# Seven block products instead of eight for the down projection in the second token half, with stored operands and gate/up products chained in PSUM

## The chip, the cores and the metric

The kernel runs on one core of a Trainium2 chip. The metric is device time in microseconds (us): the median of 3 runs of the kernel before is 1944.34 us (1938.64 to 1944.6). The profile is of one further execution.

## The reference

One transformer block over S = 2048 tokens of width D = 576, in float32.

```python
x = x + ga * attention(layernorm(x) * (1 + ca) + sa)     # 32 heads, causal in 4 segments, with a memory
h = layernorm(x) * (1 + cb) + sb                          # 2048 x 576
g = silu(h @ w_gate)                                      # 576 x 4608
u = h @ w_up                                              # 576 x 4608
x = x + gb * ((g * u) @ w_down)                           # 4608 x 576
```

The change is in the last three lines, the feed-forward part. Every float32 operand of a matmul is split into a high part in a shorter format (fp32r) and a low part, the remainder, and a product of two such operands takes three matmuls: high by high, high by low, low by high.

## The kernel before

**Stages.** Projections and attention run first and are, but for one DMA queue, not touched. Then the feed-forward part runs as two token halves t of 1024 tokens (1024 = two blocks of L = 512). In each half it walks through p = 0 to 17: NPR = 18 *periods*, each for 256 of the 4608 hidden columns. The loop `for t`, `for p`, `for k` at the end of `block` writes out by hand, in program order, what each engine does. Each engine works through its own queue strictly in that order and waits where an operand is missing or a buffer is not yet free.

**Gate and up by seven products.** A period computes the gate (z = 0) and up (z = 1) parts of 256 columns by 1024 tokens, as 2 by 2 blocks with a seven-product scheme of the Strassen kind in place of eight block products. So a period has 14 *steps* k = 0 to 13, one product m each, in the order MO7. The seven token-side operands `y[:, o]` are made once for each half. The weight-side operands are sums of the four raw blocks: `load_o` brings the raw blocks, `sum_o` (L1059, POOL) makes three new blocks and overwrites one, `prep_w` (L1065 to L1067) makes the high part on ACT, the low part `wl` on DVE and a 32-row remainder on POOL. `prod` (L1082 to L1091) then issues seven 128x512 matmuls into a PSUM bank of tag "M", which has four banks. `step` and `fin` (L1098 to L1131) combine the products *outside* PSUM: DVE adds each bank to a running sum `tx` or `ty`; gate blocks go through Silu on ACT; up blocks are multiplied with the gate blocks, and the result is split into `ah` (ACT) and `al` (DVE).

**Down by eight products.** `down` (L1141 to L1158) takes the split result of the period before and the split down weights (`load_d`, `prep_d`), and for each of eight token tiles issues 2 x 6 matmuls of 128x288 into a pair of banks of tag "dn" (two such pairs); DVE adds each pair into an accumulator `acc` (L1155). The eight pieces are spread over steps 4 to 11. The very last period's down pieces stand behind the loop.

**Beside it.** While half 0 runs, the generator `prep2` (L969 to L1038) normalises half 1's tokens, makes its seven token-side operands and stores them in HBM; it is advanced once in each of steps 4 to 13. `load_y` brings them into `y` during the last period of half 0.

**What sets the order around the change.** PSUM has 8 banks: four "M" and two pairs "dn". A list `later` holds the DVE and POOL halves of an operand's preparation and issues them one step after its ACT half. SP issues almost every DMA in program order.

## Time and profile before

| | |
|---|---|
| median of 3 runs | 1944.34 us (1938.64 to 1944.6) |
| profiled execution | span 1946.8 us; the page gives no other time for it |
| PE (matmul) busy | 1901.2 us, 98% of the span |
| DVE, POOL, ACT busy | 1533.1, 1020.6, 824.8 us (79%, 52%, 42%) |
| first gate/up product starts, last down matmul ends | 659.16 us, 1942.82 us |
| mean TensorE clock granted | 0.993 of full |

PE is TensorE, DVE VectorE, ACT ScalarE, POOL GpSimd, SP the engine that issues DMAs. A group's row gives the line, the engine, the operation, the tiles it writes and reads, the count, and then busy time in all and the mean of one in ns. Matmul records overlap: each lasts longer than the distance from its start to the next one's start, and that distance is what it costs PE. The same holds for DVE.

### The profile page before, as it was taken

Reading aid. Unit: us, or ns where it says so; the run is one execution under the profiler, and the core shown is the slowest. Engines: PE = TensorE matmul, PEld = TensorE weight load, DVE = VectorE, ACT = ScalarE, POOL = GpSimd, SP = SyncE. Lnnn points to the kernel's source line nnn. Section 1 sums busy time; section 2 is a strip of 40 time slices with the busy share of each in tenths; the row PEclk is TensorE's granted clock in tenths of the full one; section 3 lists DMA queues with packets and bytes.
Section 4 is the critical chain, followed back from the end, with each engine's and each line's share of the span. In section 5 each row is a group of like instructions: output and inputs, shape, how many; then the busy total and the mean of one; then the engine's idle time right before and its main releaser. Section 6 shows DMA issues by size and latency. Waiting matters only on the chain.

```text
span 1946.8 us, 31901 instructions
## 1 busy us (share of the span) xinstructions
PE 1901.2 (98%) x11119; PEld 1593.1 (82%) x11119; DVE 1533.1 (79%) x3218; ACT 824.8 (42%) x1652; POOL 1020.6 (52%) x1396
## 2 busy tenths in 40 slices
PE   7999999999999899999999999999999999999999
PEld 4887865676766678888888888888888888888888
DVE  6575257878786999898898988979888888878886
ACT  2222256767667434344344343433333333333332
POOL 5322235455544866556565565556565564655551
PEclk9999999999999899999999999999999999999999
DMA  7776564444443332232222222174211211112111
GB/s 207 244 227 233 203 204 140 131 139 150 136 128 125 92 135 101 89 106 80 80 106 83 82 84 78 60 264 146 74 62 45 74 62 59 60 62 74 62 57 50
DMA packets 114354, 223.59 MB, mean 115 GB/s; under 512 B 22992, under 2 KB 40784, under 8 KB 112720
## 3 DMA queue, kind: packets, MB, share of 16 engines
q1 hardware_dynamic: 111936, 215.61, 34.2%
q0 software_dynamic: 576, 5.11, 0.7%
q8 instruction: 88, 1.44, 0.3%
q10 hardware_dynamic: 1680, 0.82, 0.2%
q14 instruction: 74, 0.61, 0.1%
HBM read 161.11 MB, written 60.36 MB: 114 GB/s over the span
## 4 chain that ended last, share of the span: by engine, by line
PE 88%; DVE 4%; DMA 4%; ACT 1%; issue 1%; POOL 1%; SPq 1%; POOLq 0%; ACTq 0%; DVEq 0%
PE M L1090 39%; PE pd L1152 23%; PE pp L93 4%; PE s L576 4%; PE av L596 4%; PE s L174 4%; PE pv L93 3%; PE pw L694 2%; DMA O<-in_wgu_dram 1%; DMA mD<-mr 1%; PE pn L765 1%; PE pm L429 1%; PE px L617 1%; PE pr L346 1%; DVE y L923 1%
## 5 line engine op out<-in xcount | busy, mean ns | idle before, releaser
L1090 PE MATMUL M<-y,wh 128*128 128x512 f32 x2520 | 792.0, 393 | 5.0 <-DVE cu L1106 2.1
L1090 PEld LDWEIGHTS M<-y,wh 128*128 128x128 f32 x2520 | 473.7, 188 | 101.7 <-issue 3.9
L1067 POOL TENSOR_TENSOR wh<-O,wh 32x128 fp32r<-32x128 f32 x504 | 296.6, 593 | 423.0 <-ACT wh L1065 271.3
L1090 PE MATMUL M<-y,wl 128*128 128x512 f32 x1008 | 394.7, 392 | 0.0
L1059 POOL TENSOR_TENSOR O<-O 128x384 f32<-128x384 f32 x288 | 315.4, 1095 | 75.0 <-DMA O<-in_wgu_dram 42.9
L1152 PE MATMUL pd<-dh,ah 128*128 128x288 f32 x1152 | 340.3, 295 | 0.2 <-DVE acc L1155 0.2
L1152 PE MATMUL pd<-dl,ah 128*128 128x288 f32 x1152 | 340.3, 295 | 0.0
L1152 PE MATMUL pd<-dh,al 128*128 128x288 f32 x1152 | 340.1, 295 | 0.0
L1110 ACT CAST ah<-sg 128x512 fp32r<-128x512 f32 x144 | 89.5, 621 | 547.8 <-DVE sg L1107 422.0
L1155 DVE TENSOR_TENSOR acc<-acc,pd 128x576 f32<-128x576 f32 x288 | 216.5, 752 | 111.8 <-PE pd L1152 108.4
L1066 DVE TENSOR_TENSOR wl<-O,wh 128x256 fp32r<-128x256 f32 x504 | 286.2, 568 | 6.0 <-ACT wh L1065 5.2
L179 DVE CUSTOM_DVE_ANT_0 junk<-s,tri 128x256 bf16<-128x256 f32 (+3 forms) x512 | 228.7, 487 | 77.2 <-PE s L174 69.8
L1065 ACT CAST wh<-O 128x384 fp32r<-128x384 f32 x504 | 242.8, 507 | 0.0
L1152 PEld LDWEIGHTS pd<-dl,ah 128*128 128x128 f32 x1152 | 217.4, 189 | 11.8
L1152 PEld LDWEIGHTS pd<-dh,ah 128*128 128x128 f32 x1152 | 216.7, 188 | 11.6 <-DVE acc L1155 0.6
L579 ACT ACTIVATE Pt<-s 128x512 f32<-128x512 f32 (+1 forms) x352 | 186.5, 559 | 88.1 <-PE s L576 72.0
L1152 PEld LDWEIGHTS pd<-dh,al 128*128 128x128 f32 x1152 | 216.6, 188 | 0.0
L1090 PEld LDWEIGHTS M<-y,wl 128*128 128x128 f32 x1008 | 190.0, 188 | 29.6
L1102 ACT ACTIVATE sg<-sg 128x512 f32<-128x512 f32 x144 | 91.2, 633 | 222.7 <-DVE sg L1101 222.7
L576 PE MATMUL s<-qs,ks 110*128 110x512 f32 (+2 forms) x384 | 150.5, 409 | 5.7 <-DMA qs<-mD 4.4
L174 PE MATMUL s<-ks,qs 108*128 108x256 f32 (+3 forms) x512 | 141.2, 327 | 3.3 <-DMA ks<-kD 1.4
L583 POOL TENSOR_SCALAR_AFFINE_SELECT Pt<-Pt 128x512 f32<-128x512 f32 x128 | 81.6, 648 | 100.6 <-ACT Pt L579 100.2
(428 smaller groups left out, 2836.6 us busy)
## 6 DMA issues: line engine op xcount, KB each, us to landing
O<-in_wgu_dram SPq DMA_DIRECT2D x72, 768.0 KB
ks<-kD SPq DMA_DIRECT2D x68, 216.0 KB
qs<-qD SPq DMA_DIRECT2D x68, 216.0 KB
kD<-fh SPq DMA_DIRECT2D x16, 512.0 KB
qD<-fh SPq DMA_DIRECT2D x16, 512.0 KB
yD<-st SPq DMA_DIRECT2D x28, 256.0 KB
y<-yD SPq DMA_DIRECT2D x7, 1024.0 KB
wml<-in_w_mod_dram SPq DMA_DIRECT2D x24, 216.0 KB
```

Of the source, the lines that this page charges most:

```text
L93: nc.tensor.matmul(ps, lhsT=a, rhs=b, start=(k == 0), stop=(k == 13))
L174: nc.tensor.matmul(bank[:, n * (h - h0):n * (h - h0) + n], lhsT=qst[b][0:108, h, 128 * i:128 * i + 128], rhs=kst[b][0:108, h // 2, 0:n], s ...
L179: nc.vector.tensor_tensor_reduce(junk[:, :n], bank[:, n * (h - h0):n * (h - h0) + n], tri[:, L - n:], 1.0, -3e38, op0=ALU.add, op1=ALU.max ...
L576: nc.tensor.matmul(bank[:, n * (g - h):n * (g - h + w)].rearrange("p (a b) -> p a b", a=w), lhsT=kst[u % NB][0:110, g // 2, 128 * j:128 * ...
L579: nc.scalar.activation(pt[:, h:h + per, :n], bank[:, :n * per].rearrange("p (a b) -> p a b", a=per), AF.Exp, scale=SCALE)
L1059: nc.gpsimd.tensor_tensor(o[:, d], o[:, a], o[:, b], op=op)
L1065: nc.scalar.copy(wh, o)
L1066: later.append(lambda: nc.vector.tensor_tensor(wl, o[:, 0:2], f32(wh[:, 0:2]), op=ALU.subtract))
L1067: later.append(lambda: nc.gpsimd.tensor_tensor(wh[32:64, 2], o[32:64, 2], f32(wh[32:64, 2]), op=ALU.subtract))
L1090: nc.tensor.matmul(bank, lhsT=a, rhs=b, start=(n == 0), stop=(n == 6))
L1152: nc.tensor.matmul(pd[:, h, :288], lhsT=a[:, tk], rhs=w[:, f, sl], start=(k == 0), stop=(k == 5))
L1155: nc.vector.tensor_tensor(o, o, pd[:, :, :288], op=ALU.add)
```

## The change

In words:

- **Down, half 1.** In periods 0 to 16 of half 1 `down` uses a seven-product scheme: seven products of 512 tokens by 288 columns with 128 hidden rows each, in 14 pieces of 6 matmuls (84 in place of 96), accumulated in seven accumulators `acc[1]` to `acc[7]`; DVE adds 14 pieces in place of 8. It needs sums of the split results, `sum_a` (4 DVE adds a period), seven `ah`/`al` in place of four, and seven `dh`/`dl` of 288 columns in place of two of 576. In half 0, and for half 1's last period, `plain` issues the same 96 matmuls as before, arranged by blocks. In the last period `comb` folds the seven accumulators into the four output blocks (5 adds on DVE, 3 on POOL, of 1152 elements).
- **Operands stored.** In half 0 POOL makes the weight sums as before, and the sums of the down weights (`sum_d`), and SP stores them to HBM (`oD`, `rD`, `wdD`). In half 1 they are loaded, and POOL does none of this. The third row block of the seven gate/up operands is prepared in one piece (`prep_r`: one ACT copy and one POOL subtraction of 896 columns for each z, in place of seven small ones), so `prep_w` covers 256 columns in place of 384.
- **Chained in PSUM.** Products of one z add up in three banks: A (two buffers) takes M1, then M6, M7 and M4 on top of it; ACT copies A to B after M1, and M2 is added on top of B; C takes M5, and later M3. ACT copies A out twice (`tb`, `tc`). The DVE additions into `tx` and `ty` go, and two of the four Silu inputs are read straight from PSUM. MO7 becomes 1, 5, 6, 2, 7, 4, 3. Operands are prepared 5 steps ahead (PF) in place of 7, with 7 buffers (WR) in place of 10.
- **Smaller moves.** `prep2` transposes into the "dn" banks and has one buffer `st` in place of two; residuals are loaded at steps given by RS; `vD` is stored from ACT's queue in place of POOL's; the host call sets a smaller DMA scratch (`dynamic_dma_scratch_size=1024`).

Cut to its core:

```diff
-WR = 10
+WR = 7
+PF = 5
+NSG = 8
+CH = (1, 1, 1, 1, 2, 1, 0, 1, 1, 1, 1, 2, 1, 0)
+CH0 = (0, 1, 1, 0, 1, 1, 0, 1, 0, 1, 1, 1, 0, 0)
+RS = {(0, 5): 2, (0, 6): 4, (0, 8): 3, (0, 10): 5, (1, 9): 2, (1, 11): 3, (1, 13): 4}
+KS = (0, 1, 2, 3)
+KA = ((5, 2), (6, 4), (7, 6), (3, 8))
+ASRC = {5: (1, 1), 6: (0, 0), 7: (0, 1), 3: (1, 0)}
...
-WW = (19, 23, 25, 26, 27, 29, 30)
+WW = (19, 23, 25, 27, 30)
...
+    wdD = [dr.tile([P, 7, 288], F32, tag=f"wd{p}", name=f"wd{p}") for p in range(NF // 2)]
+    oD = [[dr.tile([P, 4, 3, P], F32, tag=f"oD{p}_{z}", name=f"oD{p}_{z}") for z in range(2)] for p in range(NF // 2)]
+    rD = [[dr.tile([96, 7, P], F32, tag=f"rD{p}_{z}", name=f"rD{p}_{z}") for z in range(2)] for p in range(NF // 2)]
...
-                nc.gpsimd.dma_start(vD[s], vs[s])
+                nc.scalar.dma_start(vD[s], vs[s])
...
-    MO7 = (1, 2, 6, 7, 4, 5, 3)
+    MO7 = (1, 5, 6, 2, 7, 4, 3)
...
-            st = x2p.tile([P, 2, 256], F32R, tag="st", name="st", bufs=2)
+            st = x2p.tile([P, 2, 256], F32R, tag="st", name="st")
...
-                    pt = ps.tile([P, 4, P], F32, tag="M", name="pt", bufs=4)
+                    pt = ps.tile([P, 2, L], F32, tag="dn", name="pt", bufs=2)[:, 0].rearrange("p (a b) -> p a b", b=P)
...
+    def load_o(t, p, z):
         O[p, z] = o = opl.tile([P, 7, 3, P], F32, tag="O", name="O", bufs=2)
+        if t == 0:
+            nc.sync.dma_start(o[:, 0:4], wgu[p, z])
+        else:
+            nc.sync.dma_start(o[:, 1:4], wgu[p, z][:, 1:4])
+            nc.sync.dma_start(o[:, 0], oD[p][z][:, 0])
+            nc.sync.dma_start(o[:, 4:7], oD[p][z][:, 1:4])
+    def store_o(p, z):
+        nc.sync.dma_start(oD[p][z][:, 0], O[p, z][:, 0])
+        nc.sync.dma_start(oD[p][z][:, 1:4], O[p, z][:, 4:7])
+    def prep_r(t, p, z):
+        R[z] = r = wrp.tile([P, 7, P], F32R, tag="wr", name="wr")
+        if t == 1:
+            nc.sync.dma_start(f32(r[0:96]), rD[p][z])
+            return
+        o = O[p, z]
+        nc.scalar.copy(r[0:96], o[0:96, :, 2, :])
+        later.append(lambda: nc.gpsimd.tensor_tensor(r[32:64], o[32:64, :, 2, :], f32(r[32:64]), op=ALU.subtract))
...
-        o = O[p, z][:, SLOT[m]]
-        wh = wp.tile([P, 3, P], F32R, tag="wh", name="wh")
+        o = O[p, z][:, SLOT[m], 0:2]
+        wh = wp.tile([P, 2, P], F32R, tag="wh", name="wh")
-        later.append(lambda: nc.vector.tensor_tensor(wl, o[:, 0:2], f32(wh[:, 0:2]), op=ALU.subtract))
-        later.append(lambda: nc.gpsimd.tensor_tensor(wh[32:64, 2], o[32:64, 2], f32(wh[32:64, 2]), op=ALU.subtract))
+        later.append(lambda: nc.vector.tensor_tensor(wl, o, f32(wh), op=ALU.subtract))
-    def load_d(p, i):
-        RD[i] = r = rp.tile([P, D], F32, tag="d", name="dr_")
-        nc.sync.dma_start(r, wd[2 * p + i])
...
+    def load_d(t, p):
+        RW[p] = r = rp.tile([P, 7, 288], F32, tag="d", name="dr_")
+        if t == 0:
+            for f in range(2):
+                nc.sync.dma_start(r[:, 2 * f:2 * f + 2].rearrange("p a b -> p (a b)"), wd[2 * p + f])
+        else:
+            nc.sync.dma_start(r[:, :NS[p]], wdD[p][:, :NS[p]])
+    def mul_d(p, f):
+        v = RW[p][:, 2 * f:2 * f + 2].rearrange("p a b -> p (a b)")
+        nc.gpsimd.tensor_tensor(v, v, gbB, op=ALU.mult)
+    def sum_d(p, j):
+        r = RW[p]
+        d, a, b = ((4, 1, 0), (5, 3, 4), (6, 2, 5), (1, 3, 1))[j]
+        nc.gpsimd.tensor_tensor(r[:, d], r[:, a], r[:, b], op=ALU.subtract)
+    def prep_d(p, key, slot):
+        r = RW[p][:, slot]
+        dh = dp.tile([P, 288], F32R, tag="dh", name="dh")
+        dl = dp.tile([P, 288], F32R, tag="dl", name="dl")
+        nc.scalar.copy(dh, r)
+        later.append(lambda: nc.vector.tensor_tensor(dl, r, f32(dh), op=ALU.subtract))
+        DP[p % 2, key] = (dh, dl)
...
+        ops.append((R[z][0:96, SLOT[m]], y[0:96, o, 4]))
-            nc.tensor.matmul(bank, lhsT=a, rhs=b, start=(n == 0), stop=(n == 6))
-        return bank
-
-    T, SG, AC = {}, {}, {}
+            nc.tensor.matmul(bank, lhsT=a, rhs=b, start=(first and n == 0), stop=(n == 6),
+                             skip_group_check=not first)
...
+            SG[ij] = g = tmp("sg", NSG)
+            if add is None:
+                nc.scalar.activation(g, bank, AF.Silu)
+            else:
+                nc.vector.tensor_tensor(g, bank, add, op=ALU.add)
+                nc.scalar.activation(g, g, AF.Silu)
+        if add is None:
+            nc.vector.tensor_tensor(g, bank, g, op=ALU.mult)
+        else:
+            u = tmp("cu", 2)
+            nc.vector.tensor_tensor(u, bank, add, op=ALU.add)
+            nc.vector.tensor_tensor(g, u, g, op=ALU.mult)
+        AC[ij] = g
+    def copy_t(tag, bank):
+        T[tag] = t = tmp(tag, 2 if tag == "cu" else 1)
+        nc.scalar.copy(t, bank)
+    B = {}
+    def step(z, m):
+        if m == 1:
+            B["A"] = ps.tile([P, L], F32, tag="A", name="A", bufs=2)
+            B["B"] = ps.tile([P, L], F32, tag="B", name="B", bufs=1)
+        elif m == 5:
+            B["C"] = ps.tile([P, L], F32, tag="C", name="C", bufs=1)
+        bank = B["B" if m == 2 else "C" if m in (5, 3) else "A"]
+        prime = "set" not in B
+        prod(z, m, bank, m in (1, 5) or m == 2 and prime, m in (2, 4, 3))
+        if m == 1:
+            if prime:
+                copy_t("cu", bank)
+            else:
+                nc.scalar.copy(B["B"], bank)
+        elif m == 2:
+            fin(z, (0, 0), bank, T["cu"] if prime else None)
+            B["set"] = True
+        elif m == 6:
+            copy_t("tb", bank)
+        elif m == 7:
+            copy_t("tc", bank)
+            fin(z, (1, 1), B["C"], T["tc"])
+        elif m == 4:
+            fin(z, (1, 0), bank)
+        elif m == 3:
+            fin(z, (0, 1), bank, T["tb"])
+    def prep_a(par, m, src):
         ah = ap_.tile([P, L], F32R, tag="ah", name="ah")
         al = ap_.tile([P, L], F32R, tag="al", name="al")
+        nc.scalar.copy(ah, src)
+        later.append(lambda: nc.vector.tensor_tensor(al, src, f32(ah), op=ALU.subtract))
+        AP[par, m] = (ah, al)
+    def sum_a(j):
+        d, a, b, op = (((1, 1), (0, 1), (1, 1), ALU.add), ((0, 1), (0, 0), (0, 1), ALU.subtract),
+                       ((0, 0), (1, 1), (0, 0), ALU.subtract), ((1, 0), (1, 0), (0, 0), ALU.subtract))[j]
+        nc.vector.tensor_tensor(PA[d], PA[a], PA[b], op=op)
+    PA, acc, x11 = {}, {}, {}
+    NS = [7] * (NPR - 1) + [4]
+    def new_acc():
+        for m in range(1, 8):
+            acc[m] = accp.tile([P, 4, 288], F32, tag=f"acc{m}", name=f"acc{m}")
...
+    def down(t, p, c):
+        m, c = POS[c // 2], c % 2
+        ah, al = AP[p % 2, m]
+        dh, dl = DP[p % 2, m]
+        pd = ps.tile([P, 2, L], F32, tag="dn", name="pd", bufs=2)
+        for i in range(2):
+            tk = slice(128 * (2 * c + i), 128 * (2 * c + i) + 128)
+            for k, (a, w) in enumerate(((ah, dh), (ah, dl), (al, dh))):
+                nc.tensor.matmul(pd[:, i, :288], lhsT=a[:, tk], rhs=w, start=(k == 0), stop=(k == 2))
+        o = acc[m][:, 2 * c:2 * c + 2]
+        if p == 0 and m not in (2, 3, 4):
+            nc.vector.tensor_copy(o, pd[:, :, :288])
         else:
+            nc.vector.tensor_tensor(o, o, pd[:, :, :288], op=ALU.add)
+    def plain(t, p, c):
+        b, h, c = c // 4, c // 2 % 2, c % 2
         pd = ps.tile([P, 2, L], F32, tag="dn", name="pd", bufs=2)
+        for i in range(2):
+            tk = slice(128 * (2 * c + i), 128 * (2 * c + i) + 128)
             k = 0
             for f in range(2):
+                ah, al = AP[p % 2, (f, b)]
+                dh, dl = DP[p % 2, (f, h)]
                 for a, w in ((ah, dh), (ah, dl), (al, dh)):
+                    nc.tensor.matmul(pd[:, i, :288], lhsT=a[:, tk], rhs=w, start=(k == 0), stop=(k == 5))
                     k += 1
+        d = x11[1] if t and b and h else acc[2 + h + 2 * b]
+        o = d[:, 2 * c:2 * c + 2]
         nc.vector.tensor_tensor(o, o, pd[:, :, :288], op=ALU.add)
+        if p == NPR - 1 and (t or c == 1):
+            store(t, b, h, d, c if t else None)
+    def comb(m):
+        def ad(eng, d, b):
+            eng.tensor_tensor(d, d, b, op=ALU.add)
+        if m == 2:
+            ad(nc.gpsimd, acc[2], acc[1])
+        elif m == 5:
+            ad(nc.gpsimd, x11[1], acc[5])
+        elif m == 6:
+            ad(nc.vector, acc[6], acc[1])
+            ad(nc.vector, acc[5], acc[6])
+        elif m == 7:
+            ad(nc.vector, acc[7], acc[6])
+            ad(nc.gpsimd, x11[1], acc[7])
+            ad(nc.vector, acc[4], acc[7])
+        elif m == 3:
+            ad(nc.vector, acc[3], acc[5])
...
+                    if n + PF < len(seq):
+                        prep_w(*seq[n + PF][1:])
+                    n += 1
                     for f in todo:
                         f()
                     step(z, m)
                     if t == 0 and p == NPR - 1 and z == 1:
                         load_y(ACT_OP[m])
+                    tn = t if nx else t + 1
+                    if not last and k == 7 - PF:
+                        load_o(tn, nx, 0)
+                    if not last and k == 14 - PF:
+                        load_o(tn, nx, 1)
+                    if tn == 0:
+                        if 5 <= k < 9:
+                            sum_o(nx, 0, k - 5)
+                        elif k >= 11:
+                            sum_o(nx, 1, k - 11)
+                    if t == 0 and k == 0 and n > 14:
+                        sum_o(p, 1, 3)
+                    if t == 0:
+                        if k == 0:
+                            store_o(p, 0)
+                        elif k == 3:
+                            store_r(p, 0)
+                        elif k == 4:
+                            store_o(p, 1)
+                        elif k == 8:
+                            store_r(p, 1)
+                    if k == 2:
+                        prep_r(t, p, 1)
+                    if not last and k == 9:
+                        prep_r(tn, nx, 0)
+                    if prev is not None and prev[0] == 0:
+                        if k == 0:
+                            prep_a(prev[1] % 2, (0, 1), PA[0, 1])
+                        if CH0[k]:
+                            plain(0, prev[1], chunk)
+                            chunk += 1
+                    elif prev is not None:
+                        for j in range(4):
+                            if k == KS[j]:
+                                sum_a(j)
+                        for j, kk in KA:
+                            if k == kk:
+                                prep_a(prev[1] % 2, j, PA[ASRC[j]])
+                        for _ in range(CH[k]):
+                            down(*prev, chunk)
+                            if last and chunk % 2:
+                                comb(POS[chunk // 2])
+                            chunk += 1
+                    if p == 0 and (t, k) in RS:
+                        load_res(t, RS[t, k])
+                    if k == 2:
+                        load_d(t, p)
+                    if t == 0:
+                        if k in (4, 5):
+                            mul_d(p, k - 4)
+                        elif k in (6, 7, 8, 11) and p < NPR - 1:
+                            sum_d(p, (6, 7, 8, 11).index(k))
+                        if k == 13:
+                            nc.sync.dma_start(wdD[p][:, :NS[p]], RW[p][:, :NS[p]])
+                    if t == 0 or last:
+                        if k in (8, 9, 10, 12):
+                            j = (8, 9, 10, 12).index(k)
+                            prep_d(p, (j // 2, j % 2), j)
+                    elif k >= 7:
+                        prep_d(p, POS[k - 7], WSLOT[POS[k - 7]])
+                    for ij, kk, j in (((0, 0), 11, 1), ((1, 1), 12, 4), ((1, 0), 13, 2)):
+                        if k == kk:
+                            prep_a(p % 2, j if t and not last else ij, AC[ij])
                     if t == 0 and k in G2 and p > 0:
                         next(g2, None)
+                PA.clear()
+                PA.update(AC)
                 prev = (t, p)
-                    if last and k == 12:
-                        flush()
-                        for i in range(LD):
-                            down(t, p, i)
-                if p == 0:
-                    load_acc(t)
...
+        flush()
+        prep_a(prev[1] % 2, (0, 1), PA[0, 1])
+        for c in range(8):
+            plain(*prev, c)
+            if c == 0:
                 flush()
-            down(*prev, i)
```

## The prediction

> **What bounds the kernel now.** I read the page's busy shares first, then its chain, then its costliest groups:
>
> ```profile
> PE 1901.2 (98%) x11119; PEld 1593.1 (82%) x11119; DVE 1533.1 (79%) x3218; ACT 824.8 (42%) x1652; POOL 1020.6 (52%) x1396
> PEclk9999999999999899999999999999999999999999
> PE 88%; DVE 4%; DMA 4%; ACT 1%; issue 1%; POOL 1%; SPq 1%; POOLq 0%; ACTq 0%; DVEq 0%
> L1059 POOL TENSOR_TENSOR O<-O 128x384 f32<-128x384 f32 x288 | 315.4, 1095 | 75.0 <-DMA O<-in_wgu_dram 42.9
> L1152 PE MATMUL pd<-dh,ah 128*128 128x288 f32 x1152 | 340.3, 295 | 0.2 <-DVE acc L1155 0.2
> L1155 DVE TENSOR_TENSOR acc<-acc,pd 128x576 f32<-128x576 f32 x288 | 216.5, 752 | 111.8 <-PE pd L1152 108.4
> L1066 DVE TENSOR_TENSOR wl<-O,wh 128x256 fp32r<-128x256 f32 x504 | 286.2, 568 | 6.0 <-ACT wh L1065 5.2
> ```
>
> The chain is PE, at full clock. What a matmul costs is the distance between starts, so next the timeline of PE in a steady period (start, duration):
>
> ```profile
> 1003.87 0.30 PE L1152 MATMUL pd<-dl,ah 128*128 128x288 f32 x1
> 1004.00 0.30 PE L1152 MATMUL pd<-dh,al 128*128 128x288 f32 x1
> 1004.14 0.40 PE L1090 MATMUL M<-y,wh 128*128 128x512 f32 x1
> 1004.37 0.39 PE L1090 MATMUL M<-y,wl 128*128 128x512 f32 x1
> ```
>
> A 288-column matmul costs 0.133 us, a 512-column one 0.230. A period is 98 x 0.230 + 96 x 0.133 = 35.3 us; 36 of them make 1271 us of the 1283.7 between the first gate/up product and the last down matmul. The waits of PE in that stretch:
>
> ```profile
> PE M L1090 <- DVE cu L1106: 2.1, 2, 1.5
> PE M L1090 <- ACT tx L1118: 1.2, 2, 1.0
> PE M L1090 <- DVE tx L1122: 1.0, 1, 1.0
> PE M L1090 <- DMA y<-yD: 0.6, 2, 0.3
> PE pd L1152 <- DVE acc L1155: 0.2, 1, 0.2
> ```
>
> So PE hardly waits: by the gaps between its starts 5.4 us in the first period (it has no down work, so DVE is late) and 2.2 us at the turn of the halves. DVE comes second. The stages, half 0, the turn and half 1 (length, then each engine's busy time, clock, DMA share, GB/s):
>
> ```profile
> 693.00:1300.00 607.00, 606.20 (x3347) 536.01 (x3348) 532.87 (x854) 242.91 (x500) 360.15 (x439) 1.00 0.29 97
> 1283.00:1310.00 27.00, 26.35 (x139) 22.38 (x138) 19.83 (x34) 7.86 (x16) 8.63 (x13) 1.00 1.02 356
> 1340.00:1930.00 590.00, 590.00 (x3257) 522.93 (x3257) 478.06 (x764) 212.87 (x426) 323.95 (x390) 1.00 0.17 59
> ```
>
> DVE is 88% busy in half 0, 81% in half 1; DMA is saturated, at 356 GB/s, only at the turn. Last, how close DVE instructions follow each other:
>
> ```profile
> 1519.62 0.76 DVE L1155 TENSOR_TENSOR acc<-acc,pd 128x576 f32<-128x576 f32 x1 [0.31 <-PE pd L1152]
> 1520.30 0.42 DVE L1066 TENSOR_TENSOR wl<-O,wh 128x256 fp32r<-128x256 f32 x1
> 1520.64 1.01 DVE L1080 TENSOR_TENSOR dl<-dr__17892,dh 128x576 fp32r<-128x576 f32 x1
> ```
>
> From start to start acc costs 0.67 and wl 0.34, 0.08 less than their records. The mean wl of 0.57 is longer because some wait for a POOL instruction in progress.
>
> **The change, part by part.**
>
> *Matmuls.* Half 1 has 84 in place of 96 down matmuls in 17 periods: 204 x 0.133 = 27.2 us less. Gate/up matmuls stay 98. This is on the path. A period of half 1 becomes 33.7 us.
>
> *DVE in half 1, against 33.7 us.* By start distances a period has 14 wl x 0.34, 14 accumulations x 0.67, 7 al x 0.61 (0.69 long), 4 sum_a x 0.61 (as al), 7 dl of 288 x 0.37 (wl plus 32 elements), and 8 instructions of fin at 0.6 to 0.7: 4.8 + 9.4 + 4.3 + 2.4 + 2.6 + 5.0 = 28.5 us, 85%. POOL has nothing to do in half 1, so no wl waits for it. It fits on average; what counts is where PE waits for DVE.
>
> *Bank C.* Before, four M banks let DVE be several products late. After, product 5 restarts the only bank C that product 3 closed just before, and DVE must have read C in between. I walk DVE's queue from the end of the last product 7 of a period. In half 1: ACT's copy tc and signals 0.66 (L1118: 0.58), cu 0.72, sg 0.61, two accumulations 1.34, wl 0.34, dl 0.37, al 0.61, fin of product 4 0.60, accumulation 0.67, wl 0.34, dl 0.37, al 0.61, read of C 0.68: 7.9 us. PE meanwhile issues four pieces of 0.8 and products 4, 3 and 1 of 1.61: 8.0, less 0.16 for the tail of product 7, so 7.9. PE waits about 0.1; with small delays I take 3 us over 17 periods (0 to 19, rival D).
>
> *Bank C in half 0.* The same walk without dl, one accumulation of two and the one after: 6.2 us, against one piece of 1.60 and three products: 6.3. But here POOL runs three sum_o (1.02 each here) and a sum_d in this stretch, and six DVE instructions with two SBUF inputs can meet them; the mean excess over the unhindered value is 0.16 for wl (579 against 415 ns in half 0), 0.06 for al, at POOL's 59%, so some 0.5 to 1 us in this dense stretch, and prep2's subtraction adds 0.4 in half the periods. Part of it falls into DVE's 0.9 us of idling ahead of tc. Ends: nothing, and 4 us if each POOL instruction there is met in full. I take 0.5 x 17 = 8.5 us, nearer to the mean excess rows than to the full collision.
>
> *First period and the stage before it.* Before: 5.4 us, since DVE had over 24 us of work in 22.5. After, DVE has some 17. But ACT's copy in prep_r at step 9 waits for POOL's fourth sum, and that for a 768 KB load queued on SP behind the store of the buffer it overwrites: by steps of 1.6 us a few us late, and tc stands behind it on ACT. I take 5 (0 to 8): -0.4. Two prep_w fewer ahead of the loop: -1 (-3 to 0).
>
> *Stores, loads and SP.* Half 0 moves 5.4 MB a period in place of 2.1, half 1 4.4 MB: 15 and 12 us at 356 GB/s, within 35. SP issues 11 to 16 DMAs a period at 0.3 to 0.45 us. Each load has 5 to 7 steps until its user. Hidden, but at the turn: there y's 8.6 MB now share the DMA engines with three loads of 1.34 MB in place of 0.77, rD and wdD, about 4 MB or 11 us more. rD's load for z = 1, issued at step 2 behind this, is needed at step 7, 12 us later. I take 4 us of PE waits in place of 2.2: +1.8 (-2 to +8).
>
> *ACT and prep2.* ACT has 17 to 19 us of work a period; its write into B has a product and a piece as cover (3.2 us in half 0), tb the same, tc one piece of 1.6 us against 0.8. `st` with one buffer makes ACT wait for a 256 KB store; the step after tc hides that. The four vD issues cost ACT 0.31 us in place of POOL's 0.6: nothing.
>
> *The end.* In the last period DVE has 28.5 - 5 wl - 3 dl + 5 adds of 1152 elements (1.29 each by the slope of wl to al) = 32.1 us, and meets three POOL adds of 2.7 us (slope of 1.02 at 384, 1.43 at 576), some 1.3 us each: 36 against 33.7. +3 (0 to 7).
>
> Sum: -27.2 + 3 + 8.5 - 0.4 - 1 + 1.8 + 3 = -12.3. The profiled execution goes from 1946.8 to 1934.5; it stands 2.5 above the median of the runs, so the median goes from 1944.3 to **1932**.
>
> **The rivals.**
>
> *B, all waits hidden.* POOL meets DVE elsewhere, the first period's waits go: -27.2 - 5.4 - 1 + 3 = -30.6: 1914. For it: DVE in half 0 drops from over 30 us to some 22. Against: the walks show no slack.
>
> *C, slower: bank C in half 0.* If DVE reads C 2.5 us late in each of 17 periods, 42 us in place of 8.5: 1966. For it: POOL is 59% busy and its sums land just there; prep_r's 896-column subtraction holds POOL about 2.1 us. Against: DVE's light load in the rest of the period. It decides from 1.6 us a period on, where the gain is gone by more than 0.3%.
>
> *D, DVE bounds half 1.* If DVE instructions cost their recorded lengths, a period sums to 32.6 us, 97%, and the 13 in the walk come 1.0 us later: 1.1 x 17 = 19 in place of 3: 1948. Against: the rows above, where the next starts 0.08 us before the record ends. The Trainium skill, "VectorE: DVE Perf Modes", section "The DRAIN you can't avoid", says that the next op does not start until the pipe empties; by that rule this rival is the forecast, 1948, and the rows at 1519.62 and 1520.30 do not agree with it.
>
> *E, the turn.* Waits of 12 us for rD and y in place of 4: 1940.
>
> **How the numbers follow.** A (1932, own range 1922 to 1942) 0.45, B 0.20, C 0.17, D 0.13, E 0.05. The range 1914 to 1956 leaves out half of B and the far part of C. About 0.3% (5.8 us) can be told from no change: faster takes most of A, B and part of E, 0.60; the same the edge of A, most of D, 0.18; slower most of C, some of D, 0.22.
>
> **What will show it.** Right: 3252 down matmuls; half 1's periods 33.7 to 33.9 us, half 0's 35.3 to 36.5, with PE's waits before product 5 of z = 0 put down to DVE's read of C; POOL idle in half 1; wl at 0.42 there. Wrong: periods of half 1 near 35, gaps before product 4 put down to ACT's tc, or PE waiting for rD loads in steady periods.

## The result, and the profile after

The changed kernel takes 1997.9 us (median of 4 runs, 1994.58 to 2001.25); the kernel before takes 1943.8 us beside it (4 runs, 1938.64 to 1944.6). The ratio is 1.028, with a 95% interval of 1.0258 to 1.0302: slower by 54 us, and outside the range of 1914 to 1956. The profiled execution of the changed kernel took 1996.87 us.

From its page, the rows that answer to those shown of before: busy shares, granted clock, the chain, and five of the costliest groups (busy us and mean ns of one, then idle time before it and its releaser).

```profile
PE 1894.5 (95%) x10915; PEld 1568.5 (79%) x10915; DVE 1494.1 (75%) x3208; ACT 931.9 (47%) x2006; POOL 658.5 (33%) x815
PEclk9999999999999899999999999999999999999998
PE 74%; DVE 15%; DMA 6%; issue 2%; POOL 2%; ACT 1%; SPq 1%; DVEq 0%; POOLq 0%; ACTq 0%
L1135 PE MATMUL C<-y,wh 128*128 128x512 f32 x576 | 209.3, 404 | 36.6 <-DVE cu L1157 36.3
L1100 DVE TENSOR_TENSOR wl<-O,wh 128x256 fp32r<-128x256 f32 x504 | 299.1, 598 | 3.3 <-ACT wh L1099 2.6
L1258 DVE TENSOR_TENSOR acc<-acc,pd 128x576 f32<-128x576 f32 x150 | 112.6, 750 | 153.5 <-PE pd L1254 153.1
L1090 POOL TENSOR_TENSOR O<-O 128x384 f32<-128x384 f32 x144 | 163.3, 1142 | 21.0 <-DVE sg L1154 5.6
L1254 PE MATMUL pd<-dh,al 128*128 128x288 f32 x608 | 182.2, 300 | 7.9 <-DVE al L1198 7.9
```

PE has 204 matmuls fewer (10915 in place of 11119), as the change says, and is busy 7 us less, but it fell from 98% to 95% of the span. In the chain DVE rose from 4% to 15%. The row of C holds the largest idle time of a matmul group: 36.3 us of waits for DVE's instruction at L1157, the read of bank C. The waits of PE (total, times, longest):

```profile
PE C L1135 <- DVE cu L1157: 36.3, 21, 3.4
PE pd L1254 <- DVE al L1198: 7.9, 4, 3.4
PE A L1135 <- DMA wr<-rD: 5.6, 2, 2.9
PE A L1135 <- ACT tc L1163: 3.6, 2, 2.4
```

And by stage, half 0 and a steady stretch of half 1 (length; busy time of PE, PEld, DVE, ACT, POOL; clock, DMA share, GB/s):

```profile
693.00:1300.00 607.00, 576.01 (x3130) 501.35 (x3129) 459.46 (x659) 266.63 (x588) 334.29 (x283) 0.99 0.48 165
1380.00:1930.00 550.00, 550.00 (x2941) 479.23 (x2940) 465.95 (x869) 264.50 (x613) 0.00 (x0) 1.00 0.43 138
```

In half 0 PE is busy 576 of 607 us, where it was busy 606.2 before. In half 1 it is busy all the time, and POOL not at all. Measured between the starts of the first products of successive periods, beside the prediction's terms for each stage (a period of half 0 as 35.3, the end as 14 products of 1.62, 14 pieces of 0.80 and 8 of 1.605):

| stage | forecast, us | measured, us | difference |
|---|---|---|---|
| start of the first gate/up product | 658.2 | 657.1 | -1.1 |
| period 0 (no down work) | 22.5 + 5 = 27.5 | 28.8 | +1.3 |
| periods 1 to 17 of half 0 | 17 x (35.3 + 0.5) = 608.6 | 16 x 38.49 + 43.27 = 659.1 | +50.5 |
| first period of half 1 (down still by eight) | 35.3 + 4 = 39.3 | 43.0 | +3.7 |
| the next 16 periods | 16 x 33.7 + 3 = 542.2 | 16 x 34.09 = 545.4 | +3.2 |
| last period and the end, to the last down matmul | 46.8 + 3 = 49.8 | 57.8 | +8.0 |

The differences add up to 65.6 us, against 62.4 between the profiled execution and its forecast (1996.87 and 1934.5); the forecast was summed from the kernel before and not from these stages. In the kernel before the six stages took 659.2, 24.1, 609.7, 37.1, 564.5 and 48.2 us (a period of half 0 35.87 in the mean of periods 1 to 16, a steady one of half 1 35.28). So the gain in half 1 is there, and half 0, which the change was to leave alone but for the preparation of operands, pays for it more than twice.

Where it is paid can be seen on the timeline of the changed kernel at the end of period 7 (start, duration): four lines of DVE, two of POOL, and the PE matmul that reopens bank C:

```profile
950.48 1.27 DVE L1125 TENSOR_TENSOR dl<-dr__11395,dh 128x288 fp32r<-128x288 f32 x1
951.67 0.68 DVE L1157 TENSOR_TENSOR cu<-C,tc 128x512 f32<-128x512 f32 x1
952.39 1.49 DVE L1158 TENSOR_TENSOR sg<-cu,sg 128x512 f32<-128x512 f32 x1
957.80 0.68 DVE L1157 TENSOR_TENSOR cu<-C,tb 128x512 f32<-128x512 f32 x1
...
950.24 1.20 POOL L1090 TENSOR_TENSOR O<-O 128x384 f32<-128x384 f32 x1
952.31 2.44 POOL L1090 TENSOR_TENSOR O<-O 128x384 f32<-128x384 f32 x2
...
958.53 0.50 PE L1135 MATMUL C<-y,wh 128*128 128x512 f32 x1 [2.35 <-DVE cu L1157]
```

Product 7 ended at 949.72, and DVE finished reading C at 958.48: 8.8 us, where the prediction walked 6.2. A `dl` of 0.45 us took 1.27 and an `sg` of 0.69 took 1.49, each beside a POOL sum. PE waited 2.35 us.

### The profile page after: what moved, and what is told of

Its sections match the earlier page's. It is cut to its first block, busy times and chain, and to the rows that moved or that the text cites. A ratio compares the mean times of both kernels' runs of the same rounds, so it can differ in the third digit from the quotient of the medians.

```text
span 1995.2 us, 30823 instructions
## 1 busy us (share of the span) xinstructions
PE 1894.5 (95%) x10915; PEld 1568.5 (79%) x10915; DVE 1494.1 (75%) x3208; ACT 931.9 (47%) x2006; POOL 658.5 (33%) x815
## 3 DMA queue, kind: packets, MB, share of 16 engines
q8 instruction: 86, 1.41, 0.3%
## 4 chain that ended last, share of the span: by engine, by line
PE 74%; DVE 15%; DMA 6%; issue 2%; POOL 2%; ACT 1%; SPq 1%; DVEq 0%; POOLq 0%; ACTq 0%
PE A L1135 17%; PE C L1135 10%; PE pd L1237 9%; PE pd L1254 8%; PE pp L101 4%; PE B L1135 4%; PE s L589 4%; PE av L609 4%; PE s L187 3%; DVE wl L1100 3%; PE pv L101 3%; PE pw L707 2%; DVE dl L1125 2%; DVE al L1198 2%; DVE acc L1258 1%
## 5 line engine op out<-in xcount | busy, mean ns | idle before, releaser
L1135 PE MATMUL A<-y,wh 128*128 128x512 f32 x1152 | 408.1, 395 | 3.6 <-ACT tc L1163 3.6
L1135 PEld LDWEIGHTS A<-y,wh 128*128 128x128 f32 x1152 | 218.2, 189 | 47.9 <-ACT tc L1163 4.5
L1135 PE MATMUL C<-y,wh 128*128 128x512 f32 x576 | 209.3, 404 | 36.6 <-DVE cu L1157 36.3
L1135 PE MATMUL A<-y,wl 128*128 128x512 f32 x576 | 228.0, 396 | 0.0
L1099 ACT CAST wh<-O 128x256 fp32r<-128x256 f32 x504 | 198.7, 402 | 0.0
L1254 PE MATMUL pd<-dh,al 128*128 128x288 f32 x608 | 182.2, 300 | 7.9 <-DVE al L1198 7.9
L1254 PE MATMUL pd<-dl,ah 128*128 128x288 f32 x608 | 181.3, 298 | 0.0
L1090 POOL TENSOR_TENSOR O<-O 128x384 f32<-128x384 f32 x144 | 163.3, 1142 | 21.0 <-DVE sg L1154 5.6
L1135 PEld LDWEIGHTS C<-y,wh 128*128 128x128 f32 x576 | 109.0, 189 | 69.7 <-DVE cu L1157 49.3
L1198 DVE TENSOR_TENSOR al<-sg,ah 128x512 fp32r<-128x512 f32 x195 | 139.8, 717 | 17.8 <-ACT ah L1197 17.6
```

What stands on the lines that cost most here:

```text
L1090: nc.gpsimd.tensor_tensor(o[:, d], o[:, a], o[:, b], op=op)
L1099: nc.scalar.copy(wh, o)
L1135: nc.tensor.matmul(bank, lhsT=a, rhs=b, start=(first and n == 0), stop=(n == 6), skip_group_check=not first)
L1198: later.append(lambda: nc.vector.tensor_tensor(al, src, f32(ah), op=ALU.subtract))
L1254: nc.tensor.matmul(pd[:, i, :288], lhsT=a[:, tk], rhs=w, start=(k == 0), stop=(k == 5))
```

## Experiments on half 0

The experiments are told by subject. They ran in this order: 1, 2, 3 and 7; then 4, 8 and 9; then 5 and 10; 11; 12; and last 6. "Mean" is the mean period of half 0's periods 1 to 16, "the wait" the mean time by which the first product 5 of these periods, which reopens bank C, starts later than the 1.62 us that product 1 takes; the changed kernel has 38.49 and 1.84 us. A time without an interval is one run beside the kernel before, which took 1939.6 to 1946.0 us in them. The changed kernel's own runs differ by up to 6.7 us, so a few us of a single time tell nothing; periods and waits were compared inside the traces.

**1. Three of POOL's sums shortened (pool_short).** They cover 8 of 128 columns; a further load fills the blocks, so the weights used are not the right ones.

```diff
-        nc.gpsimd.tensor_tensor(o[:, d], o[:, a], o[:, b], op=op)
+        w = slice(0, 8) if short else slice(0, P)
+        nc.gpsimd.tensor_tensor(o[:, d, :, w], o[:, a, :, w], o[:, b, :, w], op=op)
...
-                            sum_o(nx, 1, k - 11)
+                            sum_o(nx, 1, k - 11, True)
```

> In half 0 the three z = 1 weight sums that POOL makes in steps 11 to 13 cover 8 of 128 columns each (the output is wrong; a load fills the blocks instead). Theory Q (DVE reaches its read of bank C late because its instructions in steps 11 to 13 meet POOL's sums): the wait before product 5 at the start of half 0's periods, 1.2 to 2.6 us now, falls by 1 to 1.7 us, half 0's periods from about 38.4 to 36.8, the kernel from 1998 to about 1972. Rival T (ACT's copy tc is late because st has one buffer): no change, 1998.

Measured: 1974.69 us; mean 37.19, the wait 0.95. Three instructions a period, on an engine that PE hardly ever waits for, are worth 22 us. Half of the wait stays.

**2. prep2 three steps earlier (prep2_early).**

```diff
-G2 = (4, 5, 6, 7, 8, 9, 10, 11, 12, 13)
+G2 = (1, 2, 3, 4, 5, 6, 7, 8, 9, 10)
```

> prep2 is advanced in steps 1 to 10 in place of 4 to 13, so that none of its DVE, ACT and POOL work stands in the last three steps. Theory Q: DVE loses one 0.5 us subtraction and a POOL instruction of 0.9 us from the stretch before the read of bank C in about half of the periods: 0.3 to 0.6 us a period, 1988 to 1993. Rival T: ACT's waits for st no longer stand before tc of the last step either, so most of the wait goes: 1970 or less.

Measured: 1989.92 us; mean 38.39, the wait 1.68, so nearly nothing there. But period 17 fell from 43.27 to 37.48: what of prep2 is left over at period 17 is run in one go at its start, and with this edit less was left (one store of an operand in period 17 in place of three).

**3. Bank C read ahead of the subtractions (c_first_shift).** In step 13 of half 0 the product and its reads are issued before the low parts that step 12 left behind; the first down piece moves from step 1 to step 2.

```diff
-CH0 = (0, 1, 1, 0, 1, 1, 0, 1, 0, 1, 1, 1, 0, 0)
+CH0 = (0, 0, 1, 1, 1, 1, 0, 1, 0, 1, 1, 1, 0, 0)
...
+                    if t == 0 and k == 13:
+                        step(z, m)
                     for f in todo:
                         f()
-                    step(z, m)
+                    if not (t == 0 and k == 13):
+                        step(z, m)
```

> In step 13 of half 0 DVE reads bank C ahead of that step's wl, dl and al (1.3 us), and the first down piece of a half 0 period stands after product 6 in place of product 5, so that al has time. Theory Q: 1.3 us less wait a period and no new one, 1998 - 22 = 1976. Rival T: tc is read by an earlier instruction and stays late, the wait shrinks by less than 0.3 us a period: 1993 or more.

Measured: 1988.39 us; mean 37.72. The wait fell from 1.84 to 0.61, but what was overtaken is late in its turn: PE now waits at other products, for DVE's reads of C, for ACT's copy of A into B and for `al`.

**4. POOL's sums away from bank C (late_load).** The second operand is loaded at step 12 and summed in steps 0 to 3 of the period that uses it.

```diff
-                    if not last and k == 14 - PF:
+                    if not last and k == (14 - PF if tn else 12):
...
-                        elif k >= 11:
-                            sum_o(nx, 1, k - 11)
-                    if t == 0 and k == 0 and n > 14:
-                        sum_o(p, 1, 3)
+                    if t == 0 and k < 4 and p > 0:
+                        sum_o(p, 1, k)
```

> The complete computation. In half 0 the raw weights of z = 1 are loaded at step 12 in place of 9 and POOL sums them in steps 0 to 3 of the period that uses them, the row remainder follows at steps 4 and 5, the last down-weight sum is made at step 10: POOL is idle while DVE works towards its read of bank C. Theory Q: as the run with shortened sums, the wait before product 5 falls by about 0.9 us and half 0's periods to about 37.2: 1975 to 1980. If POOL's lateness in delivering sums mattered rather than its meetings with DVE, later sums make it worse: 2000 or more.

Measured: 2000.96 us, a miss; mean 38.19. The wait fell to 1.20, but the sums now meet the subtractions `al` that the first down piece needs: between 700 and 1290 us PE waits 9.0 us for `al`, where it waited 0.4. Moving the meeting moves the wait. Period 0 is longer too, 32.2 us in place of 28.8.

**5. Three staging tiles for prep2 (st_three),** with m going round 1, 6 and 7.

```diff
-            st = x2p.tile([P, 2, 256], F32R, tag="st", name="st")
+            m = sb.pop(0)
+            sb.append(m)
+            st = acc[m].rearrange("p a b -> p (a b)")[:, :512].rearrange("p (a b) -> p a b", b=256).bitcast(F32R)
```

> The changed kernel, with the token-side operands' staging tile st taken in turn from three accumulators that the first half does not use yet (1, 6 and 7), so ACT need not wait for the 256 KB store of the one before. In the profile of the changed kernel ACT waits for that store 15 times, 31.6 us in all. Theory (meetings of DVE and POOL on the way to the read of bank C, with the store's wait mostly hidden): that ACT wait falls under 5 us, half 0's mean period only from 38.49 to 38.1, the time to 1987 to 1993. Rival T (the one-buffer staging tile makes the copy of product 7 late, and that is what bank C waits for): the wait before product 5 falls from 1.84 to under 1.0 us a period, time 1970 to 1980.

Measured: 1998.31 us; mean 38.61, the wait 2.10. ACT's waits for the store (31.6 us) are gone and nothing is gained: in the changed kernel something else is always later. Both forecasts had it faster.

**6. The prices apart (pool_off, prep2_last, both_off).** Four mends had each taken a part, so these three take the suspects out altogether. POOL's work of half 0 on 8 columns:

```diff
-        nc.gpsimd.tensor_tensor(o[:, d], o[:, a], o[:, b], op=op)
+        w = slice(0, 8)
+        nc.gpsimd.tensor_tensor(o[:, d, :, w], o[:, a, :, w], o[:, b, :, w], op=op)
...
-        nc.gpsimd.tensor_tensor(v, v, gbB, op=ALU.mult)
+        nc.gpsimd.tensor_tensor(v[:, 0:8], v[:, 0:8], gbB[:, 0:8], op=ALU.mult)
...
-        nc.gpsimd.tensor_tensor(r[:, d], r[:, a], r[:, b], op=ALU.subtract)
+        nc.gpsimd.tensor_tensor(r[:, d, 0:8], r[:, a, 0:8], r[:, b, 0:8], op=ALU.subtract)
```

and prep2 out of periods 1 to 16:

```diff
-G2 = (4, 5, 6, 7, 8, 9, 10, 11, 12, 13)
+G2 = ()
```

> The changed kernel with every POOL instruction of the periods of half 0 (sum_o, sum_d, mul_d and the subtraction into wr) on 8 columns only; more loads fill the blocks that are then not computed (some 1.6 MB a period more to load in half 0), and the gate/up and down weights used are not the right ones. Theory (POOL in DVE's way is nearly all of it; the walk of 6.2 us is right without POOL): wl comes back to 0.42 us in half 0, the wait before product 5 falls from 1.84 to under 0.4 us a period, half 0's mean period from 38.49 to 35.7 to 36.4, time 1950 to 1962. Rival (the walk was too short by itself): the wait before product 5 stays above 0.8, mean above 36.9, time above 1970.

> The changed kernel with none of prep2 in periods 1 to 16; all of it runs at the start of period 17, which grows by a few hundred us, so only periods 1 to 16 are compared, not the time. Theory (prep2 is a minor part): mean period from 38.49 to 37.3 to 38.0, the wait before product 5 to 1.2 to 1.6. Rival (prep2's instructions in ACT's, DVE's and SP's queues are the main part): mean under 36.5, the wait under 0.6.

> Both of these at once; again only periods 1 to 16 count. If the walk of DVE's queue is right when nothing disturbs it (6.2 us against PE's 6.3), the wait before product 5 is 0 to 0.2 us and the mean period 35.5 to 35.7 (14 x 1.62 + 8 x 1.605 = 35.5). If the walk left something out, the wait before product 5 stays at 0.4 or more in nearly every period, mean 36 or more.

Measured, over periods 1 to 15 (in the two kernels without prep2 the gap of period 17's work already falls into period 16):

| | mean period, us | the wait, us |
|---|---|---|
| changed kernel | 38.35 | 1.81 |
| prep2_last: POOL alone | 36.90 | 1.41 |
| pool_off: prep2 alone | 36.35 | 0.39 |
| both_off: neither | 35.49 | 0.00 |

The whole time of pool_off is 1944.4 us, beside 1939.62 of the kernel before, but 7 us of its gain lie ahead of the first gate/up product, where sums are shortened too; the other two times mean nothing. The mean of prep2_last is below the range expected for it. The two waits add up to the third (1.41 + 0.39 = 1.80), and with neither there is none: the walk of 6.2 us was right for an undisturbed queue. The periods do not add up so neatly: POOL costs 1.41 and prep2 0.86 us, both together 2.86.

The same piece of a period in the two kernels shows the mechanism. First prep2_last (POOL as in the changed kernel), lines of DVE, POOL and PE:

```profile
790.83 1.68 DVE L1100 TENSOR_TENSOR wl<-O,wh 128x256 fp32r<-128x256 f32 x1
792.44 1.27 DVE L1125 TENSOR_TENSOR dl<-dr__9799,dh 128x288 fp32r<-128x288 f32 x1
794.89 0.95 DVE L1100 TENSOR_TENSOR wl<-O,wh 128x256 fp32r<-128x256 f32 x1
795.76 1.28 DVE L1125 TENSOR_TENSOR dl<-dr__9799,dh 128x288 fp32r<-128x288 f32 x1
796.97 0.68 DVE L1157 TENSOR_TENSOR cu<-C,tc 128x512 f32<-128x512 f32 x1
801.90 0.68 DVE L1157 TENSOR_TENSOR cu<-C,tb 128x512 f32<-128x512 f32 x1
...
790.12 2.11 POOL L1085 TENSOR_TENSOR wr<-O,wr 32x896 fp32r<-32x896 f32 x1 [3.85 <-issue]
794.55 3.37 POOL L1090 TENSOR_TENSOR O<-O 128x384 f32<-128x384 f32 x3
...
802.64 0.50 PE L1135 MATMUL C<-y,wh 128*128 128x512 f32 x1 [1.27 <-DVE cu L1157]
```

Then both_off:

```profile
777.80 0.42 DVE L1102 TENSOR_TENSOR wl<-O,wh 128x256 fp32r<-128x256 f32 x1
778.13 0.45 DVE L1129 TENSOR_TENSOR dl<-dr__9817,dh 128x288 fp32r<-128x288 f32 x1
781.00 0.42 DVE L1102 TENSOR_TENSOR wl<-O,wh 128x256 fp32r<-128x256 f32 x1
781.33 0.46 DVE L1129 TENSOR_TENSOR dl<-dr__9817,dh 128x288 fp32r<-128x288 f32 x1
782.61 0.69 DVE L1161 TENSOR_TENSOR cu<-C,tc 128x512 f32<-128x512 f32 x1 [0.82 <-ACT tc L1167]
787.45 0.69 DVE L1161 TENSOR_TENSOR cu<-C,tb 128x512 f32<-128x512 f32 x1
...
788.19 0.50 PE L1139 MATMUL C<-y,wh 128*128 128x512 f32 x1
```

From `cu` with tc to the read of C it is 4.93 us in the one (796.97 to 801.90) and 4.84 in the other (782.61 to 787.45): there POOL alone does no harm. The harm lies ahead of it. In both_off DVE stands idle for 0.82 us until tc comes. In prep2_last the two `wl` and two `dl` of steps 10 to 12 take 5.18 us in place of 1.75; the idle time is eaten up, and DVE begins the walk late.

In the changed kernel, where POOL and prep2 come together, the walk itself grows too. In the mean of periods 1 to 15 DVE starts `cu` 1.37 us after tc is ready (0.03 in both_off, 1.27 in prep2_last), and from there to `cu` with tb it takes 5.88 us (4.84 in both_off, 4.94 with POOL alone, 5.25 with prep2 alone): an `al` of up to 1.50 and an `sg` of up to 1.49 us meet POOL in it, and prep2's instructions stand in it. Two other suspects fall away. ACT is not late: it starts tc 0.06 us after product 7 ends. Nor is it the larger transfers: pool_off moves 222 GB/s in half 0 (693 to 1260 us) against 165 in the changed kernel, and hardly waits.

The Trainium skill, "SBUF — State Buffer", section "SBUF: two separate sides", says that DVE and GpSimd share a pair of SBUF ports by an exclusive lock, which a DVE instruction with two SBUF inputs needs too, and that whichever comes second waits for the whole instruction of the other. The traces agree: `wl` and `dl`, with two SBUF inputs, grow by up to 1.26 us, and `acc` and `cu`, with one input in PSUM, keep their 0.74 to 0.76 and 0.68 us.

## Experiments on half 1, the turn and the end

**7. Half 1 with eight products again (plain_half1).** `down` of half 1 is taken by `plain`, 96 matmuls a period; all else stays, the stored and loaded operands too. In half 1 the second block of the down weights is then the stored difference and not the weights.

```diff
-                    if prev is not None and prev[0] == 0:
+                    if prev is not None:
...
-                            plain(0, prev[1], chunk)
+                            plain(*prev, chunk)
```

> Half 1 computes its down product as half 0 does, with 96 matmuls a period; all else stays. The 204 matmuls cost 27.2 us. If half 1's seven products gain what the profile shows (periods of 34.1 against 35.3) and the folding at the end costs 8 to 11 us, this is 1998 + 17 x 1.2 - 10 = 2008. If DVE bounds half 1 with seven products, it is 1998 or less.

Measured: 2022.01 us; half 1's periods 35.48 in place of 34.09, the last period and the end 50.1 in place of 57.8. So the seven products gain 1.39 us a period, 1.39 x 16 = 22.2 in the periods measured, and the last period and the end give 7.7 of it back. The rest of the 25 us to the changed kernel's time lies ahead of half 1, in stages that the edit does not touch (the first product starts 4.6 us later, half 0's mean is 0.36 us longer), so it is no price of the edit.

**8. The end and the turn (tail_turn).** The additions into the accumulators for products 7 and 3 go between the last down pieces, and the loads of `rD` come two steps earlier.

```diff
+                    if k == 7 and not last and (t or p == NPR - 1):
+                        prep_r(1, nx, 0)
...
-                            if last and chunk % 2:
+                            if last and chunk % 2 and POS[chunk // 2] not in (7, 3):
...
+                comb(3)
+            elif c == 1:
+                comb(7)
```

> The complete computation. The four folding adds for products 7 and 3 move from the last period to the places between the down pieces behind the loop, and half 1's row remainders are loaded two steps earlier, ahead of y's loads at the turn. Theory Q: the last stretch, 57.8 us from the last period's start to the last matmul against 46.5 of issue, loses 6 to 9 us, the turn 5.6 us of waits for rD: 1983 to 1988. If the end waits for the matmul operands' ACT and DVE chain itself, under 3 us.

Measured: 1991.2 us. The first period of half 1 fell from 42.98 to 36.08 and the end from 57.8 to 52.35: 12.3 us. The time fell by 5.7, since stages that the edit doesn't touch were longer in this run (the first product starts 2.6 us later, period 0 takes 1.1 and half 0's 16 periods 2.7 us more). The end of the changed kernel, lines of POOL, DVE and PE, shows what was mended:

```profile
1967.15 3.72 POOL L1264 TENSOR_TENSOR x<-x,acc 128x1152 f32<-128x1152 f32 x1 [10.30 <-DVE acc L1264]
1968.98 2.44 DVE L1198 TENSOR_TENSOR al<-sg,ah 128x512 fp32r<-128x512 f32 x1
1971.47 0.61 PE L1254 MATMUL pd<-dh,al 128*128 128x288 f32 x1 [1.76 <-DVE al L1198]
1972.71 1.36 DVE L1264 TENSOR_TENSOR acc<-acc,acc 128x1152 f32<-128x1152 f32 x1
1977.03 0.61 PE L1254 MATMUL pd<-dh,al 128*128 128x288 f32 x1 [3.40 <-DVE al L1198]
```

An `al` of 0.69 us took 2.44 beside a POOL addition of 3.72, and the additions on DVE stand ahead of the `al` on which the last pieces wait.

## Experiments that put the mends together

**9. half0 and all1.** half0 is late_load with c_first_shift and prep2 in steps 0 to 10; all1 is half0 with tail_turn.

```diff
-G2 = (4, 5, 6, 7, 8, 9, 10, 11, 12, 13)
+G2 = (0, 1, 2, 3, 4, 5, 6, 7, 8, 9, 10)
```

> The late load, prep2 in steps 0 to 10 and the early read of bank C with the shifted piece, all in half 0. Theory Q: the three act on one stretch, each takes its part and together they leave less than 0.3 us before product 5; periods 35.7 to 36.3: 1952 to 1962. If the wait before product 5 only stands for DVE being full over the whole period, it comes up before other products and the periods stay above 37: 1975 or more.

> Both of the former: 1937 to 1950, the sum of the two gains, if the stretches are independent.

Measured: half0 1974.01 us (mean 37.28, the wait 0.36, period 17 at 35.44), all1 1964.32 us. Both are above what was expected. Single periods are long in all1 (42.2 us in period 6, 39.7 in period 7, 40.1 in period 13), with most of the others at 35.3 to 36.8. Its period 6, two lines of ACT and one of PE:

```profile
887.19 0.40 ACT L991 CAST st<-t 128x256 fp32r<-128x256 f32 x1 [6.55 <-DMA yD<-st]
887.81 0.58 ACT L1163 COPY tc<-A 128x512 f32<-128x512 f32 x1
888.43 0.79 PE L1135 MATMUL A<-y,wh 128*128 128x512 f32 x1 [3.62 <-ACT tc L1163]
```

ACT stood 6.55 us for the 256 KB store of the one staging tile, which was issued on SP behind a load of 768 KB and two of 288 KB; the copy tc is queued behind it, and PE waits for tc.

**10. all_st: all1 with the staging tiles of st_three.**

```diff
-            st = x2p.tile([P, 2, 256], F32R, tag="st", name="st")
+            m = sb.pop(0)
+            sb.append(m)
...
```

> The kernel with all of the mends so far (time 1964.3), with the three staging tiles of st_three as well. Its remaining excess in half 0 is 1.8 us a period over the 35.5 of its matmuls, and sits in single periods (42.2, 39.7, 38.2, 40.1, 39.1) in which ACT stood up to 6.5 us for the store of st while the copy of product 7 or 6 was queued behind it. Theory T for this remainder: ACT's wait for the store (55 us) goes, the single long periods come down to 36 to 37.5, half 0's mean to 36.0 to 36.4, time 1943 to 1950. Rival (the long periods come from POOL, which stands up to 12.7 us for the load of wd and then gives its sums and wr late): mean period stays above 36.9, time 1957 to 1964.

Measured: 1950.94 us; mean 36.65, a little above what was expected; period 6 at 35.88. The edit that gained nothing in the changed kernel gains 13 us here. What is left is this, early in period 11 (DVE, POOL, PE):

```profile
1055.68 1.50 DVE L1201 TENSOR_TENSOR al<-sg,ah 128x512 fp32r<-128x512 f32 x1
1058.26 1.48 DVE L1201 TENSOR_TENSOR al<-sg,ah 128x512 fp32r<-128x512 f32 x1
...
1055.41 3.78 POOL L1093 TENSOR_TENSOR O<-O 128x384 f32<-128x384 f32 x3
...
1059.79 0.61 PE L1257 MATMUL pd<-dh,al 128*128 128x288 f32 x1 [2.04 <-DVE al L1201]
```

Two `al` of 0.68 us took 1.50 and 1.48 beside three POOL sums, and the first down piece waited 2.04 us for `al`.

**11. all2: the second operand's sums in steps 2 to 5, the first down piece in step 3, the end's additions a piece later.**

```diff
-CH0 = (0, 0, 1, 1, 1, 1, 0, 1, 0, 1, 1, 1, 0, 0)
+CH0 = (0, 0, 0, 1, 1, 1, 1, 1, 0, 1, 1, 1, 0, 0)
...
-                    if t == 0 and k < 4 and p > 0:
-                        sum_o(p, 1, k)
+                    if t == 0 and 2 <= k < 6 and p > 0:
+                        sum_o(p, 1, k - 2)
```

> all_st (1950.9) with three orders changed: the second operand's sums on POOL in steps 2 to 5 instead of 0 to 3 and the first down block in step 3 instead of 2 (in all_st the sums met the subtractions of the low parts in steps 0 to 2: 1.24 us for a wl, 1.50 for an al, and the block in step 2 waited up to 3.1 us for al, 0.67 us a period on average); period 0's load of wd two steps earlier (POOL stands 16.5 us for it and the period takes 32.3 us where the changed kernel took 28.8); the additions of the end placed one piece later each. Theory (meetings with POOL ahead of step 2): half 0's mean period falls from 36.65 to 35.8 to 36.1, period 0 to 28 to 30, the end by 1 to 3 us: 1933 to 1940, below the 1943.3 of the kernel before. Rival (the sums meet other DVE work wherever they stand, and the wait only moves to another product): mean 36.5 to 36.9, 1945 to 1950.

Measured: 1959.53 us, a miss; mean 37.18. The first down piece no longer waits for `al`, but the subtraction into `wr` now comes behind the products with wd, which wait for their load, and between 690 and 1300 us PE waits 15.5 us for `wr`. The end grew to 54.6 us.

**12. all3: all2 with the products with wd two steps later, the sums and `wr` ahead of them, the end as in all_st.**

```diff
-                        if k in (4, 5):
-                            mul_d(p, k - 4)
-                        elif k in (6, 7, 8, 10) and p < NPR - 1:
-                            sum_d(p, (6, 7, 8, 10).index(k))
+                        if k in (6, 7):
+                            mul_d(p, k - 6)
+                        elif k in (8, 9, 10, 11) and p < NPR - 1:
+                            sum_d(p, k - 8)
```

> all2 (1959.5) with POOL's order mended: there the first down block no longer waited for al, but wr, whose subtraction on POOL stood behind the two products with wd and their load, was late (PE waited 15.5 us in nine places before product 1 and 5). Here the two products with wd come two steps later, the second operand's sums and wr ahead of them, and the additions of the end are back where all_st had them. Theory (half 0 loses where a result of POOL or DVE is queued behind a wait, and nothing else): half 0's mean period falls from 37.18 to 35.8 to 36.3, period 0 from 31.6 to 24 to 28, end 52.3, time 1930 to 1940. Rival (POOL's and DVE's meetings cost the same wherever the work stands): mean 36.5 to 37.0, time 1945 to 1953.

Measured: 1942.73 us (median of 9 runs, 1938.03 to 1947.28) beside 1945.1 (12 runs, 1941.06 to 1948.83); the ratio is 0.9983, with an interval of 0.9971 to 0.9996. The median is a little above the range expected; the mean of 36.26 is in its range and period 0 at 28.33 us is just above it. Order, with three staging tiles for prep2 in place of one, takes the change from 2.8% slower to level with the kernel before. The matmuls, operands and transfers are those of the changed kernel; its busy row says the same of the engines:

```profile
PE 1886.2 (97%) x10915; PEld 1568.1 (81%) x10915; DVE 1481.4 (76%) x3208; ACT 930.5 (48%) x2006; POOL 657.0 (34%) x815
```

It has the change's gain in half 1 (periods of 34.09 against 35.28 before, 19 us over 16) and pays most of it back in half 0 (36.26 against 35.87, 6 us over 16), at period 0 (28.3 against 24.1) and at the end (52.3 against 48.2). One period of half 0, p = 15, takes 40.4 us, with waits of 2.12 us for C and 1.02 for `al`.

## Why the prediction was wrong

*Bank C in half 0* is the step that failed: "I take 0.5 x 17 = 8.5 us". The wait was 1.84 us a period, 31 us over 17 periods, and a period lost 2.9 us in all (38.35 against 35.49 in both_off). The place and the mechanism were right: PE waits before product 5 of z = 0 for DVE's read of C, behind DVE instructions that met POOL. The mis-sized term is the meetings. The prediction priced them by the mean excess in the kernel before (0.16 us for a `wl`), counted them from the start of the walk on, and let DVE's idle time ahead of tc take a part. Experiment 6 shows that most of POOL's fall ahead of the walk, 3.4 us of them in one stretch of two `wl` and two `dl`, and use that idle time up (1.3 us a period in the mean); POOL and prep2 together add another 1.0 us inside the walk. The rows of `wl` in half 0 (690 to 1290 us), first of the changed kernel, then of pool_off:

```profile
L1100 DVE TENSOR_TENSOR wl<-O,wh 128x256 fp32r<-128x256 f32 x220 | 168.9, 776 | 0.4
L1102 DVE TENSOR_TENSOR wl<-O,wh 128x256 fp32r<-128x256 f32 x230 | 95.2, 423 | 1.3 <-issue 0.5 <-ACT wh L1101 0.4
```

So a `wl` takes 0.78 us in the mean against 0.42 with POOL short: an excess of 0.36, twice that of before, though POOL is busy 334 of 607 us against 360. Why it doubled was not shown. Rival C, with 2.5 us a period and 1966 us, had the cause; its point of decision, 1.6 us a period, was passed. Its time was still 32 us too low, since the steps below failed as well.

*ACT and prep2* was costed at nothing: "`st` with one buffer makes ACT wait for a 256 KB store; the step after tc hides that". For `st` that holds in the changed kernel (experiment 5), and fails as soon as the other waits are shorter: 13 us between all1 and all_st. For the rest of prep2 it does not hold: 0.86 us a period beside no POOL at all, 1.45 beside POOL (38.35 - 36.90), and the 7.8 us by which period 17, where its remainder is run at once, exceeds the 35.44 that it takes in half0 with prep2 in steps 0 to 10. Of the 0.86 us, 0.28 are prep2's transposes on PE itself, 48 matmuls of 0.09 us each; the kernel before has them too, so they are no part of the loss: its periods of half 0 take 35.3 us without them and 35.7 to 36.2 with them.

*The end*: +3 was taken; the last period and the end cost 11 us over their matmuls. The meeting with a POOL addition was foreseen with 1.3 us; it took 1.75 of an `al`, and DVE's queue ahead of the last `al`, with one more addition of 1.36 us in it, another 3.4, which the step did not look at.

*The turn*: 4 us of waits were taken. The first period of half 1 was 7.7 us over its 35.3. The loads of `rD` made PE wait 5.6 us, as the step feared; issued two steps earlier, they leave 36.08.

*The clock* had no term at all: long waits of PE are followed by stretches at half rate, some 11 us of the loss (last section).

*First period*: 5 us of waits were taken; it ran 6.3 us over its 22.5 us of matmuls. The 5.4 us that the prediction read for this period in the kernel before lie only in part there: period 0 took 24.1 us, 1.6 over, and period 1 39.1, 3.8 over. *The stage before*: -1 was taken, -2.1 measured, which says nothing: in the other kernels that share this stage the first product starts anywhere from 655.0 to 663.1 us.

*Matmuls* and *DVE in half 1* were right in the main. Periods of half 1 are 34.09 us, a little above the 33.7 to 33.9 forecast; they gain 1.19 us on the 35.28 of the kernel before, 19 us over 16 periods, where 1.6 was taken. PE waits for C about 0.2 us a period there (*Bank C* took 3 us over 17 periods); the other 0.2 was not traced. POOL idles there, and DVE is busy 85% (465.95 of 550 us), as forecast. The row of `wl` in half 1 of the changed kernel:

```profile
L1100 DVE TENSOR_TENSOR wl<-O,wh 128x256 fp32r<-128x256 f32 x236 | 98.3, 417 | 0.0
```

So rival D, DVE as the bound of half 1 by full record lengths, fell. The section of the Trainium skill that the prediction names for it, "The DRAIN you can't avoid", goes on that a next op that is not held starts earlier; the prediction left that out, and the rows at 1519.62 and 1520.30 agree with it. B, all waits hidden, fell with half 0; of E, the price of the turn was right in kind (7.7 us against the 12 it named).
